# Giving out the half differences of a max search one row half at a time, in an attention mix on one core

## The chip, the core and the metric

The kernel runs on one core of one Trainium2 chip. The metric is the device time of one execution, in microseconds (us). The profile is of one execution, recorded instruction by instruction. Engines are named as the profile names them: PE is TensorE's matmuls and PEld its weight loads, ACT is ScalarE, DVE is VectorE, POOL is GpSimd, SP is SyncE.

## The reference: what is computed

Two attention branches share one input x of 2048 positions by 512 features and are mixed by a sigmoid gate. Branch A is a sliding, dilated attention: 32 heads of 16 features, each query against 8 keys, two positions apart. Branch B is a full attention with 32 query heads and one shared key head and value head. The output is the gated sum.

```python
scores = jnp.einsum("bhqd,bkd->bhqk", q, k) * (Dh ** -0.5)
p = _softmax(scores, axis=-1)
o = jnp.einsum("bhqk,bkd->bhqd", p, v)
...
return g * a + (1 - g) * b
```

The softmax of branch B needs, for every query and head, the maximum of its scores over 2048 keys (or a number near it), and finding these maxima is the work that the change is about.

## The kernel before, in words

**The work of branch B.** It is cut into 32 units (NU), each of 512 queries and four heads. The weighted part runs in 512 steps, 16 a unit: a step takes 128 keys, forms the scores of the unit by two pairs of matmuls (`exp_pair`, L487; the four heads lie in pairs of 64-row halves of the array, even in rows 0 to 63, odd in rows 64 to 127), exponentiates them with two ACT instructions (L489), and multiplies the result of the step before with the values (`weighted`, L497, eight matmul instructions a step).

**The maxima.** Before a unit's step 0 the maxima of its rows have to be known, since they are fed into the score matmul as an additional row of the queries. They are found by "fills": a score matmul of 128 queries by 512 keys, for an even or an odd head, into a bank of PSUM, and a DVE maximum over it. One row half by 512 keys is a half fill; there are 2048 of them (NF). Three forms exist:

- `fill_pair`: both halves, matmuls into the two banks of m2 (tile pm), one DVE reduce of 1024 (L357).
- `fill_one`: one half into m1 (tile ps) or po, one DVE reduce of 512 (L368).
- The difference form, which covers four half fills (two blocks of 512 keys, both heads). It uses max(a, b) = (a + b)/2 + |a - b|/2. `half_keys` and `half_parts` prepare the half sums and half differences of pairs of key blocks (kcd) once. `fill_diff` issues two half matmuls of differences (L422) into the two banks of m2, and two ACT absolute values (L432) from there into the halves of a tile dd. Two half sums follow (`fill_sum`): a half matmul (L422) into m1 for even and po for odd, and one DVE instruction (L442) that adds the absolute values to it, writes the sum back over them in dd, and keeps the maximum.

`half_sel` makes one dd tile for the projection stage; an output stage takes two tiles of the exponentials' pool (pexp) instead, and `dd.append(dd.pop(0))` turns to the other one for each difference.

**The stages.** First the keys, queries and branch A's projections are formed. From some 26 us on, the rest of the queries (14 lumps) and branch A's projections (64 lumps, L1098, each of 12 rounds; a round is one matmul in each row half) run as a stream; ACT copies each finished lump out of PSUM (L251, L252), POOL adds the halves, and a DMA on SP's queue stores every second one to ad. The difference form is used from 100 us on, when kcd is formed. From 266 us on the 512 steps run, with plain fills between the matmuls. Two output stages interrupt the steps, for eight and for four rows of the output: streams of projection matmuls (L783) in which fills run in the difference form again. The last four rows are spread over the last steps. POOL computes branch A beside all this. At most eight units' queries fit in SBUF, so fills reach only units 0 to 7 before the steps begin.

**What sets the order.** The kernel is scheduled by hand: the Python planner keeps a clock for PE, ACT and DVE (`clk`) and the time at which each bank comes free (`free`), adds its constants (T_R 0.23 for a round, 0.18 where it is a branch A round, T_LAT 0.20, T_TTR 0.66 and so on), and writes instructions in the order in which this clock says that they can run. The hardware runs each engine's queue in that order and waits on semaphores where the clock was wrong. `stream` is the planner's loop for the projection and output stages. In each pass it may give one row half to a single fill or a half sum (`single`), while the other half, or both, goes on with the stream. At the end of a pass it may issue a whole round besides: `fill_diff` if a pair of key blocks is at hand, no half sum is pending, m2 is free and DVE's clock is at most 1.2 us ahead. Half sums (`pend`) go out in order, when their bank is free and their absolute value will be ready within 0.4 us (`ready_d`). After an output stage, pending half sums are drained.

In the main loop the planner places `fill_pair` and `fill_one` by the banks' clocks; an output stage begins at a unit's start when its rows' attention is done and the fills are less than LEAD = 3 units ahead.

Of the kernel before, what the change touches and what calls it, by code (L numbers as in the profile page):

```python
# [8 lines left out]
AF = mybir.ActivationFunctionType  # L9
ALU = mybir.AluOpType  # L10
# [29 lines left out]
FMAX = 3.4028234e38  # L40
NH = NJ // 2
TO_END = 10
LEAD, M2S, M1S, E1S, PER_ROW = 3.0, 0.5, 0.3, 0.2, 20


T_R, T_LAT, T_EXP, T_RED2, T_RED1, T_W, T_TTR = 0.23, 0.20, 0.92, 1.14, 0.61, 1.21, 0.66
# [3 lines left out]
def gated_mix_kernel(ctx, tc, xt, wa, wk, wq, wo_a, wo_b, out):  # L50
    nc = tc.nc
# [20 lines left out]
    def home(v):  # L72

        return (v % NB, v - NB) if v < 2 * NB - 2 else ((v - NB) % (NB - 2), v - NB + 2)
# [3 lines left out]
    m2 = pp.tile([P, 2, 512], F32, name="pm")  # L78
    m1 = pp.tile([P, 512], F32, name="ps")
    po = pp.tile([P, 512], F32, name="po")  # L80
# [5 lines left out]
    clk = {"pe": 0.0, "act": 0.0, "dve": 0.0}  # L86

    def after(eng, ready, dur):
        clk[eng] = max(clk[eng], ready) + dur
        return clk[eng]  # L90
# [214 lines left out]
    slots = [(v, pr, t, kc) for kc in range(2) for v in range(2) for pr in range(2) for t in range(4)]  # L305
    slots += [(v, pr, t, kc) for v in range(2) for pr in range(2) for t in range(4) for kc in range(2, 4)]
    slots += [(v, pr, t, kc) for v in range(2, NU) for pr in range(2) for t in range(4) for kc in range(4)]
    half = []
    free = {"m2": 0.0, "m1": 0.0, "e0": 0.0, "e1": 0.0, "po": 0.0}
# [3 lines left out]
    def fillable():  # L313
        return bool(half) or bool(slots) and slots[0][0] < len(stacked) and stacked[slots[0][0]] <= clk["pe"]

    def unit_tile(v):
        for x in (v, v + 1):
            if x < NU and x not in left:
                mx[x] = wp.tile([P, 2, 2, 4, 4], F32, name="mx", bufs=3)
                if pe:  # L320
                    nc.gpsimd.memset(mx[x], -FMAX)
                    charge(250)
                else:
                    nc.scalar.activation(mx[x].rearrange("p b i t k -> p (b i t k)"), ident[:, 0:64], AF.Identity, scale=0.0, bias=mk[:, 6:7])
                left[x] = NF // NU
        return mx[v]

    def max_mm(dst, v, pr, t, kc, odd):
        b = 64 * odd
        nc.tensor.matmul(dst, qst[home(v)[0]][b:b + 62, pr, t * P:(t + 1) * P], kst[b:b + 62, kc * 512:(kc + 1) * 512], start=True, stop=True)  # L330
# [30 lines left out]
    def fill_one(dst=m1, key="m1"):  # L361
        if not half:
            v, pr, t, kc = slots.pop(0)
            half.extend([(v, pr, t, kc, 0), (v, pr, t, kc, 1)])
        v, pr, t, kc, odd = half.pop(0)
        m = unit_tile(v)
        max_mm(dst, v, pr, t, kc, odd)
        nc.vector.tensor_reduce(m[:, odd, pr, t, kc:kc + 1], dst, AX.X, ALU.max)  # L368
        free[key] = after("dve", after("pe", 0, T_R) + T_LAT, T_RED1) + 0.08
        filled(v, 1)  # L370


    sel, kcd, dd, pend, ready_d, formed, ended, wants = [], [], [], [], [0.0, 0.0], set(), set(), []
# [43 lines left out]
    def paired():  # L417
        return len(slots) > 1 and slots[0][3] % 2 == 0 and slots[0][3] // 2 in formed and slots[1] == slots[0][:3] + (slots[0][3] + 1,) and fillable()

    def half_mm(dst, v, pr, t, kc, x, odd):  # L420
        b = 64 * odd
        nc.tensor.matmul(dst, qst[home(v)[0]][b:b + 62, pr, t * P:(t + 1) * P], kcd[0][b:b + 62, kc // 2, x, :], start=True, stop=True)  # L422

    def fill_diff():
        v, pr, t, kc = slots.pop(0)
        slots.pop(0)
        for odd in range(2):
            half_mm(m2[:, odd, :], v, pr, t, kc, 1, odd)
        at = after("pe", 0, T_R) + T_LAT
        dd.append(dd.pop(0))  # L430
        for odd in range(2):
            nc.scalar.activation(dd[0][:, odd], m2[:, odd, :], AF.Abs)  # L432
            ready_d[odd] = after("act", at, 0.52) + 0.1
        free["m2"] = ready_d[1]
        pend.extend([(v, pr, t, kc, 0), (v, pr, t, kc, 1)])

    def fill_sum():
        v, pr, t, kc, odd = pend.pop(0)
        m = unit_tile(v)
        dst, key = ((m1, "m1"), (po, "po"))[odd]  # L440
        half_mm(dst, v, pr, t, kc, 0, odd)
        nc.vector.tensor_tensor_reduce(dd[0][:, odd], dst, dd[0][:, odd], 1.0, -FMAX, ALU.add, ALU.max, m[:, odd, pr, t, kc:kc + 1])  # L442
        free[key] = after("dve", max(clk["pe"] + T_R + T_LAT, ready_d[odd]), T_TTR) + 0.08
        filled(v, 2)

# [34 lines left out]
    pe, pexp, exped = [], {}, {}  # L480
# [251 lines left out]
    def stream(seq, mm, done, pooled):  # L732

        at, told = [0, 0], 0
        ended.clear()
        while min(at) < len(seq):
            single, odd = None, -1
            if wants and all(free[k] <= clk["pe"] + 0.1 for k in (("m1", "po") if wants[0] else ("m2",))):
                half_keys(wants.pop(0))
            if pend:  # L740
                if free[("m1", "po")[pend[0][4]]] <= clk["pe"] + 0.1 and ready_d[pend[0][4]] <= clk["pe"] + 0.4:
                    single, odd = fill_sum, pend[0][4]
            elif paired() and not half or 1 in wants:
                pass
            elif fillable() and free["m1"] <= clk["pe"] + 0.1:
                single, odd = lambda: fill_one(m1, "m1"), half[0][4] if half else 0
            elif pooled and fillable() and free["po"] <= clk["pe"] + 0.1:
                single, odd = lambda: fill_one(po, "po"), half[0][4] if half else 0
            dur = 0.0
            for b in (0, 1) if odd != 1 else (1, 0):  # L750
                if b == odd:
                    now = clk["pe"]
                    single()
                    clk["pe"] = now
                elif at[b] < len(seq):
                    dur = mm(b, seq[at[b]])
                    at[b] += 1
            after("pe", 0, dur or T_R)
            if ended or 0 in wants:
                pass  # L760
            elif paired():
                if not half and not pend and max(free["m2"], clk["dve"] - 1.2) <= clk["pe"] + 0.1:
                    fill_diff()
            elif slots and fillable() and free["m2"] <= clk["pe"] + 0.1:
                clk["pe"] = max(clk["pe"], free["m2"])
                fill_pair(m2, "m2")
            while told < min(at):
                told += 1
                done(seq[told - 1])

    def out_phase(js, n, whole_unit):

        m = 3 * (C + n)
        items = {}

        def mm(b, at):
            x, j, i = at
            if j not in items:
                items[j] = out_items(j, n)
                clk["pe"] = max(clk["pe"], free[f"e{x % 2}"])  # L780
            st, mv = items[j][i]
            h = slice(64 * b, 64 * b + 64)
            nc.tensor.matmul(eb[x % 2][:, b, :], st()[h], mv[h], start=(i == 0), stop=(i == m - 1))  # L783
            return T_R

        def done(at):
            x, j, i = at
            if i % 4 == 3:
                run_tasks()
                run_pool()  # L790
            if x == len(js) - 1 and i == m - 5:
                ended.add(1)
            if x == 0 and i == 1:
                turn(j, 1)
            if x == 0 and i == 6:
                later.pop(j)()
            if i == 3 * n and j != js[-1]:
                prepare(js[x + 1], n)
            if i == m - 5 and j != js[-1]:
                turn(js[x + 1], 1 - x % 2)  # L800
            if i == m - 1:
                out_store(j, x % 2)
                if j != js[-1]:
                    later.pop(js[x + 1])()

        if whole_unit:
            formed.update((0, 1))
            free["po"] = max(free["po"], clk["dve"] + 0.1)
            dd[:] = [px.tile([P, 2, 512], F32, name="pexp", bufs=6) for _ in range(2)]
        stream([(x, j, i) for x, j in enumerate(js) for i in range(m)], mm, done, False)  # L810
        while pend:
            odd = pend[0][4]
            clk["pe"] = max(clk["pe"], free[("m1", "po")[odd]], ready_d[odd] - 0.3)
            fill_sum()
            clk["pe"] += T_R
        settle("sum", 0)
        formed.clear()
# [329 lines left out]
    for s in range(NS + 1):  # L1147
# [11 lines left out]
        v = min(x[0][0] for x in (half, slots, [(NU,)]) if x)  # L1159
# [114 lines left out]
```

## Time and profile before

| | |
|---|---|
| median of 3 runs | 1475.5 us (1475.44 to 1475.64) |
| profiled execution | 1475.43 us |
| span, first to last instruction | 1473.6 us |
| granted TensorE clock | 0.999 |
| projection stage with differences | 100 to 266 us |
| steps before the first output stage | 266 to 846 us |
| output stages | 846 to 914 us and 1185 to 1222 us |
| difference absolute values (L432) | 164 in dd, 108 in pexp |

A line of the page's groups reads: line of the kernel, engine, operation, output tile <- input tiles, shape, count | busy us, mean ns of one | idle time of the engine before them, and what ended it. A line of the windows reads: stretch, its length, then per engine busy us and count of instructions, then the granted clock, the share of the DMA engines and GB/s. A line of the timeline reads: start, length, engine, line, operation, tiles, count of merged instructions, and idle time before with its releaser.

### The profile page before, as it was taken

To read this page: it belongs to the slowest core of one execution; us is meant where nothing else is said; L and a number is where in the kernel's file an instruction comes from. 1 tells how busy PE (TensorE), PEld (TensorE's weight loads), DVE (VectorE), ACT (ScalarE), POOL (GpSimd) and SP (SyncE) were. 2 spreads that over 40 slices of the span, in tenths; PEclk is the share of its full clock that TensorE was granted. 3 is DMA by queue.
4 is the path that set the end of the run, shared out by engine and by line. 5 is a ranking of instruction groups with operands and counts; after the bars stand their busy time and mean duration, and the time that the engine had idled before them with its cause. 6 is when DMAs were issued, how large, how long until landed. Compare 5 with 4: busy or idle time off the path is not lost.

```text
span 1473.6 us, 29548 instructions
## 1 busy us (share of the span) xinstructions
PE 1461.7 (99%) x10996; PEld 708.0 (48%) x10996; DVE 1193.9 (81%) x1855; ACT 1274.5 (86%) x1646; POOL 1032.6 (70%) x1828
## 2 busy tenths in 40 slices
PE   9999999999999999999999999999999999999998
PEld 5999889533333333333333376333333364333333
DVE  6976667789888888888898878899888878889712
ACT  5468988899999999999999978999999988999986
POOL 7876988887888979888889898888888330111220
PEclk9999999999999999999999999999999999999999
DMA  6754323121220211202112121120120000000110
GB/s 224 209 151 136 93 88 120 34 85 42 66 80 7 85 60 42 71 12 71 45 38 77 36 64 67 42 71 26 57 71 12 12 27 16 13 1 2 29 31 30
DMA packets 54080, 89.86 MB, mean 61 GB/s; under 512 B 18800, under 2 KB 35232, under 8 KB 49712
## 3 DMA queue, kind: packets, MB, share of 16 engines
q1 hardware_dynamic: 46928, 48.99, 11.4%
q0 software_dynamic: 6432, 37.94, 7.8%
q8 instruction: 86, 1.41, 0.4%
q10 hardware_dynamic: 576, 1.05, 0.2%
q14 instruction: 58, 0.48, 0.1%
HBM read 60.07 MB, written 27.35 MB: 59 GB/s over the span
## 4 chain that ended last, share of the span: by engine, by line
PE 91%; ACT 3%; POOL 3%; issue 1%; DVE 1%; DMA 1%; DVEq 0%; POOLq 0%; ACTq 0%
PE po L497 35%; PE pe L487 23%; PE pm L330 8%; PE ps L330 7%; PE pe L1098 7%; PE pe L783 4%; PE pm L422 2%; PE ps L422 1%; PE pm L851 1%; ACT dd L432 1%; PE po L422 1%; POOL qlo L222 1%; POOL qraw L215 1%; PE pe L185 1%; DMA xraw<-xt 1%
## 5 line engine op out<-in xcount | busy, mean ns | idle before, releaser
L489 ACT ACTIVATE pexp<-pe 128x1024 f32<-128x1024 f32 x1022 | 989.5, 1022 | 93.0 <-PE pe L487 90.8
L357 DVE TENSOR_REDUCE mx<-pm 128x2 f32<-128x1024 f32 x495 | 605.8, 1224 | 117.6 <-PE pm L330 113.8
L497 PE MATMUL po<-pexp,vst 128*32 128x512 f32 x4096 | 545.7, 605 | 0.0
L487 PE MATMUL pe<-qst,kst 64*128 64x512 f32 x1916 | 434.5, 447 | 0.4 <-ACT pexp L489 0.3
L487 PEld LDWEIGHTS pe<-qst,kst 64*128 64x128 f32 x1916 | 179.7, 183 | 473.7 <-ACT pexp L489 467.8
L368 DVE TENSOR_REDUCE mx<-ps 128x1 f32<-128x512 f32 x481 | 327.1, 680 | 3.7 <-PE ps L330 3.7
L330 PE MATMUL pm<-kst,qst 62*128 62x512 f32 x945 | 192.0, 396 | 0.3 <-DVE mx L357 0.3
L561 POOL TENSOR_TENSOR pr<-aext 128x256 f32<-128x256 f32 x256 | 182.5, 738 | 2.2 <-DMA aext<-ad 1.9
L330 PE MATMUL ps<-kst,qst 62*128 62x512 f32 x455 | 180.0, 396 | 0.2 <-DVE mx L442 0.2
L621 POOL TENSOR_TENSOR oa<-oa,av 128x256 f32<-128x256 f32 x224 | 164.1, 732 | 15.1
L497 PEld LDWEIGHTS po<-pexp,vst 128*32 128x32 f32 x4096 | 80.8, 108 | 178.2 <-issue 169.1
L618 POOL TENSOR_TENSOR av<-aext,lg 128x256 f32<-128x256 f32 x224 | 139.3, 622 | 12.7
L1098 PE MATMUL pe<-wah,xh 64*128 64x384 f32 (+1 forms) x504 | 109.8, 338 | 0.4 <-ACT gate L255 0.4
L1098 PE MATMUL pe<-wal,xh 64*128 64x384 f32 (+1 forms) x504 | 110.1, 337 | 0.0
L1098 PE MATMUL pe<-wah,xl 64*128 64x384 f32 (+1 forms) x504 | 109.9, 337 | 0.0
L432 ACT ACTIVATE dd<-pm 128x512 f32<-128x512 f32 x164 | 91.0, 608 | 17.8 <-PE pm L422 11.3
L442 DVE CUSTOM_DVE_ANT_0 dd<-ps,dd 128x512 f32<-128x512 f32 x82 | 56.7, 692 | 55.1 <-PE ps L422 28.9
L330 PEld LDWEIGHTS pm<-kst,qst 62*128 62x128 f32 x945 | 92.0, 187 | 2.8 <-DVE mx L357 1.0
L330 PEld LDWEIGHTS ps<-kst,qst 62*128 62x128 f32 x455 | 85.0, 187 | 5.5 <-DVE mx L368 1.7
L567 POOL TENSOR_TENSOR tr<-pr 128x512 f32<-128x512 f32 x64 | 81.7, 1277 | 4.1
L567 POOL TENSOR_TENSOR tr<-tr 128x256 f32<-128x256 f32 (+1 forms) x128 | 72.4, 566 | 8.3
L524 POOL TENSOR_TENSOR rl<-rl,gate_t 128x16 f32<-128x16 f32 x31 | 6.8, 220 | 100.4 <-DVE rl L518 99.9
(215 smaller groups left out, 1896.2 us busy)
## 6 DMA issues: line engine op xcount, KB each, us to landing
aext<-ad POOLq DMA_DIRECT2D x32, 1056.0 KB, 5.5
ad<-stage SPq DMA_DIRECT2D x32, 384.0 KB
qst<-qd SPq DMA_DIRECT2D x60, 128.0 KB
xraw<-xt SPq DMA_DIRECT2D x16, 256.0 KB
qd<-qhi SPq DMA_DIRECT2D x16, 256.0 KB
qd<-qlo SPq DMA_DIRECT2D x16, 256.0 KB
qst<-qd SPq DMA_DIRECT2D x60, 64.0 KB
qst<-ml SPq DMA_DIRECT2D x216, 2.0 KB
```

Of the source, the lines that this page charges most:

```text
L330: nc.tensor.matmul(dst, qst[home(v)[0]][b:b + 62, pr, t * P:(t + 1) * P], kst[b:b + 62, kc * 512:(kc + 1) * 512], start=True, stop=True)
L357: nc.vector.tensor_reduce(m[:, :, pr, t, kc], dst, AX.X, ALU.max)
L368: nc.vector.tensor_reduce(m[:, odd, pr, t, kc:kc + 1], dst, AX.X, ALU.max)
L432: nc.scalar.activation(dd[0][:, odd], m2[:, odd, :], AF.Abs)
L487: nc.tensor.matmul(bank[:, odd, :], kst[b:b + 64, kt * P:(kt + 1) * P], qst[home(u)[0]][b:b + 64, pr, :], start=True, stop=True)
L489: nc.scalar.activation(e, bank, AF.Exp, scale=SCALE)
L497: nc.tensor.matmul(po[32 * i:32 * i + 32, :], vst[:, kt, :], pexp[s, i // 2][:, i % 2, :], start=(kt == 0), stop=(kt == NJ - 1))
L561: nc.gpsimd.tensor_mul(pr[:, k], q, e[:, o:o + NH, AC:2 * AC])
L567: nc.gpsimd.tensor_add(nx, cur[:, :, 0:n], cur[:, :, n:2 * n])
L618: nc.gpsimd.tensor_mul(av, e[:, o:o + NH, 2 * AC:].rearrange("p j (h d) -> p j h d", d=DH), lg[:, w].unsqueeze(3).to_broadcast([P, NH, AG, ...
L621: nc.gpsimd.tensor_add(ao, ao, av)
L1098: nc.tensor.matmul(front[2 if x == last else x % 2][0][:, b, :n], l[h], r[h], start=(i == 0), stop=(i == 3 * C - 1))
```

## The change

`fill_diff` no longer issues both halves. It issues one: the even half opens a pair (`open_group`), the odd half completes it. The new `diff_half` says which half may go: its own bank has to be free (`half_free`, by the planner's clock, with the margin M2H = 0.0), no half sum of the same half may be pending, and DVE's clock may be at most 1.6 us ahead. A half difference takes its row half's turn in a pass of the stream, like a half sum, while the other half goes on with the stream or with a half sum; before, the pair was a round of its own. A difference may thus go out while the other half's sum is pending. Each pending half sum carries the tile of its own difference (`d`) instead of using the current `dd[0]`. The absolute value is charged 0.54 instead of 0.52. At the end of an output stage an open pair is completed first.

```diff
+M2H = 0.0
...
+    open_group, half_free = [], [0.0, 0.0]
+
+    def diff_half():
+
+        if max(half_free) != free["m2"]:
+            half_free[:] = [free["m2"]] * 2
+        odd = len(open_group) and 1
+        if any(x[4] == odd for x in pend) or half_free[odd] > clk["pe"] - M2H or clk["dve"] - 1.6 > clk["pe"]:
+            return None
+        return odd
+
     def fill_diff():
-        v, pr, t, kc = slots.pop(0)
-        slots.pop(0)
-        for odd in range(2):
-            half_mm(m2[:, odd, :], v, pr, t, kc, 1, odd)
-        at = after("pe", 0, T_R) + T_LAT
-        dd.append(dd.pop(0))
-        for odd in range(2):
-            nc.scalar.activation(dd[0][:, odd], m2[:, odd, :], AF.Abs)
-            ready_d[odd] = after("act", at, 0.52) + 0.1
-        free["m2"] = ready_d[1]
-        pend.extend([(v, pr, t, kc, 0), (v, pr, t, kc, 1)])
+        if not open_group:
+            open_group.append(slots.pop(0))
+            slots.pop(0)
+            dd.append(dd.pop(0))
+            odd = 0
+        else:
+            odd = 1
+        v, pr, t, kc = open_group[0]
+        half_mm(m2[:, odd, :], v, pr, t, kc, 1, odd)
+        nc.scalar.activation(dd[0][:, odd], m2[:, odd, :], AF.Abs)
+        half_free[odd] = ready_d[odd] = after("act", clk["pe"] + T_R + T_LAT, 0.54) + 0.1
+        free["m2"] = max(half_free)
+        pend.append((v, pr, t, kc, odd, dd[0]))
+        if odd:
+            open_group.clear()
 
     def fill_sum():
-        v, pr, t, kc, odd = pend.pop(0)
+        v, pr, t, kc, odd, d = pend.pop(0)
         m = unit_tile(v)
         dst, key = ((m1, "m1"), (po, "po"))[odd]
         half_mm(dst, v, pr, t, kc, 0, odd)
-        nc.vector.tensor_tensor_reduce(dd[0][:, odd], dst, dd[0][:, odd], 1.0, -FMAX, ALU.add, ALU.max, m[:, odd, pr, t, kc:kc + 1])
+        nc.vector.tensor_tensor_reduce(d[:, odd], dst, d[:, odd], 1.0, -FMAX, ALU.add, ALU.max, m[:, odd, pr, t, kc:kc + 1])
...
             if pend:
                 if free[("m1", "po")[pend[0][4]]] <= clk["pe"] + 0.1 and ready_d[pend[0][4]] <= clk["pe"] + 0.4:
-                    single, odd = fill_sum, pend[0][4]
-            elif paired() and not half or 1 in wants:
+                    lone[pend[0][4]] = fill_sum
+            elif open_group or paired() and not half or 1 in wants:
                 pass
...
+            if open_group or paired() and not (ended or half or 0 in wants):
+                odd = diff_half()
+                if odd is not None and odd not in lone:
+                    lone[odd] = fill_diff
             dur = 0.0
-            for b in (0, 1) if odd != 1 else (1, 0):
-                if b == odd:
+            for b in sorted((0, 1), key=lambda b: b not in lone):
+                if b in lone:
                     now = clk["pe"]
-                    single()
+                    lone[b]()
                     clk["pe"] = now
                 elif at[b] < len(seq):
                     dur = mm(b, seq[at[b]])
                     at[b] += 1
             after("pe", 0, dur or T_R)
-            if ended or 0 in wants:
-                pass
-            elif paired():
-                if not half and not pend and max(free["m2"], clk["dve"] - 1.2) <= clk["pe"] + 0.1:
-                    fill_diff()
-            elif slots and fillable() and free["m2"] <= clk["pe"] + 0.1:
+            if not (ended or 0 in wants or open_group or paired()) and slots and fillable() and free["m2"] <= clk["pe"] + 0.1:
                 clk["pe"] = max(clk["pe"], free["m2"])
                 fill_pair(m2, "m2")
...
         stream([(x, j, i) for x, j in enumerate(js) for i in range(m)], mm, done, False)
+        if open_group:
+            clk["pe"] = max(clk["pe"], half_free[1], free["m2"])
+            fill_diff()
+            clk["pe"] += T_R
```

More of the change, by code (lines that the diff above doesn't have):

```diff
@@ L736, in stream @@
         while min(at) < len(seq):
-            single, odd = None, -1
+            lone = {}
             if wants and all(free[k] <= clk["pe"] + 0.1 for k in (("m1", "po") if wants[0] else ("m2",))):
@@ L741, in stream @@
                 if free[("m1", "po")[pend[0][4]]] <= clk["pe"] + 0.1 and ready_d[pend[0][4]] <= clk["pe"] + 0.4:
-                    single, odd = fill_sum, pend[0][4]
-            elif paired() and not half or 1 in wants:
+                    lone[pend[0][4]] = fill_sum
+            elif open_group or paired() and not half or 1 in wants:
                 pass
             elif fillable() and free["m1"] <= clk["pe"] + 0.1:
-                single, odd = lambda: fill_one(m1, "m1"), half[0][4] if half else 0
+                lone[half[0][4] if half else 0] = lambda: fill_one(m1, "m1")
             elif pooled and fillable() and free["po"] <= clk["pe"] + 0.1:
-                single, odd = lambda: fill_one(po, "po"), half[0][4] if half else 0
+                lone[half[0][4] if half else 0] = lambda: fill_one(po, "po")
+            if open_group or paired() and not (ended or half or 0 in wants):
+                odd = diff_half()
+                if odd is not None and odd not in lone:
+                    lone[odd] = fill_diff
             dur = 0.0
-            for b in (0, 1) if odd != 1 else (1, 0):
-                if b == odd:
+            for b in sorted((0, 1), key=lambda b: b not in lone):
+                if b in lone:
                     now = clk["pe"]
-                    single()
+                    lone[b]()
                     clk["pe"] = now
```

## The prediction, made before the changed kernel was run

> **What bounds the kernel now.** I read the page first (busy shares, chain, groups), then the windows of each stage, then the timelines of one stretch of the projection stage and one of the main loop. The page:
>
> ```profile
> span 1473.6 us, 29548 instructions
> PE 1461.7 (99%) x10996; PEld 708.0 (48%) x10996; DVE 1193.9 (81%) x1855; ACT 1274.5 (86%) x1646; POOL 1032.6 (70%) x1828
> PE 91%; ACT 3%; POOL 3%; issue 1%; DVE 1%; DMA 1%; DVEq 0%; POOLq 0%; ACTq 0%
> L432 ACT ACTIVATE dd<-pm 128x512 f32<-128x512 f32 x164 | 91.0, 608 | 17.8 <-PE pm L422 11.3
> L442 DVE CUSTOM_DVE_ANT_0 dd<-ps,dd 128x512 f32<-128x512 f32 x82 | 56.7, 692 | 55.1 <-PE ps L422 28.9
> ```
>
> TensorE is busy nearly throughout and carries 91% of the chain, so what counts is TensorE rounds and the moments when it stands still. The 164 absolute values (L432) in tile dd are 82 differences in the projection stage, from 100 to 266 us; the other 108, in tiles pexp, are 54 differences in the two output stages. Each difference (four half matmuls, two absolute values, two reduces) replaces four plain fills.
>
> The later 24 projection lumps, 192.6 to 265.3 us, from three views of that stretch (the copy line L251, the projection matmuls L1098, the absolute values L432):
>
> ```profile
> 192.60:265.30 72.70, 11.69 (x24) 1.00 0.33 102
> 192.60:265.30 72.70, 65.74 (x576) 60.59 (x576) 1.00 0.33 102
> 192.60:265.30 72.70, 42.23 (x76) 1.00 0.33 102
> 126.10:192.60 66.50, 10.78 (x23) 1.00 0.38 118
> 126.10:192.60 66.50, 36.47 (x66) 1.00 0.38 118
> ```
>
> That is 24 lumps of 3.03 us with 38 differences, 1.58 a lump; the 23 lumps before hold 33, so 71 differences in 47 lumps, 1.51 a lump. Now the timeline of two differences:
>
> ```profile
> 167.84 0.69 DVE L442 CUSTOM_DVE_ANT_0 dd<-ps,dd 128x512 f32<-128x512 f32 x1 [0.83 <-PE ps L422]
> 168.23 0.42 PE L422 MATMUL pm<-kcd,qst 62*128 62x512 f32 x2
> 168.46 0.68 DVE L442 CUSTOM_DVE_ANT_0 dd<-po,dd 128x512 f32<-128x512 f32 x1
> 168.47 0.36 PE L1098 MATMUL pe<-wah,xl 64*128 64x384 f32 x2
> 168.65 0.35 PE L1098 MATMUL pe<-wah,xh 64*128 64x384 f32 x2
> 168.69 1.10 ACT L432 ACTIVATE dd<-pm 128x512 f32<-128x512 f32 x2 [0.45 <-PE pm L422]
> 168.99 0.39 PE L422 MATMUL ps<-kcd,qst 62*128 62x512 f32 x1
> 169.53 0.69 DVE L442 CUSTOM_DVE_ANT_0 dd<-ps,dd 128x512 f32<-128x512 f32 x1 [0.38 <-PE ps L422]
> 169.83 0.19 PEld L422 LDWEIGHTS pm<-kcd,qst 62*128 62x128 f32 x2 [0.25 <-ACT dd L432]
> 169.84 0.51 PE L422 MATMUL pm<-kcd,qst 62*128 62x512 f32 x2
> 170.18 0.34 PE L1098 MATMUL pe<-wah,xl 64*128 64x384 f32 x2
> ```
>
> Three things are to be seen. **Round prices:** a pair of projection matmuls takes 0.18 us (168.47 to 168.65), a pair of 512-column fills 0.24 (168.23 to 168.47); I use 0.176 and 0.23, since some starts lie closer. The 24 lumps then need 576/2 x 0.176 + 38 x 4/2 x 0.23 = 50.7 + 17.5 = 68.2 us; of 72.7, so 4.5 us, or **0.19 us a lump, are stalls**. **Bank wait:** the second difference's weight load at 169.83 waited 0.25 us for the absolute values, which end at 168.69 + 1.10 = 169.79; its pair then costs 0.34 instead of 0.23. **The buffer chain:** the reduce that starts at 168.46 ends at 169.14; it reads and rewrites the odd half of dd. The second absolute value of the 1.10 us pair ends at 169.79, and with one lasting 0.60 (the group's mean is 608 ns) it began near 169.19: 0.05 after that reduce ended. The projection stage has one dd tile (half_sel makes one), so absolute value, reduce and next absolute value of one half form a chain. The waits of this stretch name it:
>
> ```profile
> ACT dd L432 <- DVE mx L442: 5.9, 8, 0.9
> PEld pm L422 <- ACT dd L432: 11.3, 39, 0.7
> ```
>
> The first is small because ACT usually arrives just in time.
>
> In the main loop (one step has two exponentials) the stretch between the projection and the first output stage, by exponentials and by plain fill matmuls, then two steps without fills from the timeline, and the page's row of the exponentials:
>
> ```profile
> 266.00:846.00 580.00, 528.40 (x546) 1.00 0.17 53
> 266.00:846.00 580.00, 206.15 (x791) 99.32 (x791) 1.00 0.17 53
> 269.27 3.79 ACT L489 ACTIVATE pexp<-pe 128x1024 f32<-128x1024 f32 x4
> L489 ACT ACTIVATE pexp<-pe 128x1024 f32<-128x1024 f32 x1022 | 989.5, 1022 | 93.0 <-PE pe L487 90.8
> ```
>
> 546 exponentials are 273 steps of 2.125 us with 791/273 = 2.9 half fills each. Four exponentials without fills take 3.79 us; one lasts 1.02, so the fourth starts 2.77 us after the first, 0.92 apart, 1.85 a step. So 2.9 halves cost 0.275 us, 0.095 each: **a difference made elsewhere saves the main loop 4 x 0.095 = 0.38 us**.
>
> **The change, part by part.** No instruction is added or removed in kind; the planner, which writes the order by its own clock, hands them out differently.
>
> *More differences per lump.* Now a pair is planned when pend is empty, m2 is free and the pair's two absolute values end; by the code's constants that is 1.49 us at the earliest. With the change each half waits for its own bank: 0.23 + 0.20 + 0.54 + 0.1 = 1.07, so six rounds of 0.18, with the reduces allowing 2 x 0.66 = 1.32. ACT becomes the planner's limit: in a lump of 12 rounds at 0.18 plus 0.36 a difference, it fits 0.8 of copies and 1.08 a difference: 1.08 n + 0.8 = 2.16 + 0.36 n, n = 1.89. Working one lump through by hand gave the repeating order d0, d1, five rounds later s0, then d0 and s1 in one round, d1, s0, next lump: two differences a lump, slipping one round a lump. With uncharged work (the splits of wah, branch A's exponentials) I take 1.75; bounds 1.51 (nothing gained) and 1.89. So 82 - 71 = 11 more differences in 47 lumps (0 to 18). The first lumps with wider rows plan 1.2 of copies and gain nothing that matters. TensorE: 11 x 2 x 0.23 = **+5.1 us** (0 to +8.3). The queries of eight units, 512 halves, cap this; it is not reached.
>
> *Stalls.* In that order d of the same half comes two differences after s, with 8 rounds between: three of 0.23 and five of 0.176 on that half, 1.57 us. What really has to happen between: s to its reduce 0.54 (168.99 to 169.53), reduce 0.69, 0.05, absolute value 0.60, then load and refill 0.16 (169.79 to the pair's useful start, 0.05 + 0.11): 2.04. So TensorE, which works its queue in order with both row halves behind one waiting load, stalls 0.47, about 0.5 us. The planner knows nothing of it: it charges the bank and ACT, not dd, and its gate lets the difference go with up to 1.6 us of VectorE work ahead. The slip by a round a lump relaxes it, 0.5, 0.3, 0.1; the mean is 0.3, and I add 0.02 for exposed loads: 0.32 against 0.19, 47 x 0.13 = **+6.1 us**. Bounds: no stall left, 47 x -0.19 = -8.9; every lump at 0.5, 47 x 0.31 = +14.6. Behind a waiting load stand the projection matmuls, then the copies L251 and L252, POOL's additions and the DMAs to ad; these have slack, since branch A reads ad only after a whole group of lumps.
>
> *Half sums bound to their own tile.* It matters in the output stages, with two dd tiles from pexp: no chain between successive differences there. Their views:
>
> ```profile
> 846.00:914.00 68.00, 39.20 (x72) 1.00 0.14 47
> 1185.00:1222.00 37.00, 19.65 (x36) 1.00 0.09 29
> ACT pexp L432 <- PE pm L422: 12.2, 20, 1.2
> ```
>
> 54 differences in 12 rows, 4.5 a row, and ACT idle 12.2 us for TensorE in the first. The same planner balance gives at most 5.5 a row. I take +7 (0 to +12): 7 x 0.46 = **+3.2 us** (0 to +5.5), stalls unchanged.
>
> *Given back.* 18 differences x 0.38 = **-6.8 us** in the main loop (0 to -11.4). It comes as steps with few fills: early, since only eight units' queries are loaded until step 17 and the fills run out there, and late, where the fills end sooner. The last four rows' products stay late, since they wait for unit 29. The drain of an open pair adds under 1 us per output stage, hidden in the 7.
>
> A page gives another reading of the last term. The Trainium skill, "Perfetto Trace Analysis", Identifying the Most-Contended Engine, says that matmul busy time is a bad measure and that weight-load share shows TensorE's headroom.
>
> ```profile
> 266.00:846.00 580.00, 579.63 (x4089) 210.31 (x4087) 512.66 (x644) 533.46 (x570) 494.65 (x945) 1.00 0.17 53
> ```
>
> Weight loads here are 210.31/580 = 36%, ACT 92%: were ACT the bound, fewer fills would save nothing and -6.8 would be 0. By that rule this stretch has headroom; the trace disagrees, since steps without fills ran at 1.85 against 2.125.
>
> **The sum.** 5.1 + 6.1 + 3.2 - 6.8 = +7.6 us. The profiled execution took 1475.43 (span 1473.6 and 1.8 around it), the median 1475.5: the same within 0.1. Forecast **1483.0**.
>
> **Rivals.**
>
> 1. *The stalls go* (faster). If a half really starts when its bank is free, the 0.19 a lump falls away: 5.1 - 8.9 + 3.2 - 6.8 = -7.4, **1468.0**. For it: the 39 bank waits. Against: the reduce that ends 0.05 us before the next absolute value. It decides if the reduce of a half ends before the next half's absolute value would start anyway. 0.16.
>
> 2. *Little changes.* The planner gives out no more than now, or the stalls stay at 0.19: 0 to 5.1 + 3.2 - 6.8 = +1.5, **1475.5 to 1477.0**. For it: the gain and cost of a difference (0.38 and 0.46) nearly cancel. This is also the case that the change does nothing. 0.22.
>
> 3. *The chain binds every lump* (slower still). 0.5 of stall in all 47: 5.1 + 14.6 + 3.2 - 6.8 = +16.1, **1491.6**. For it: the repeating order. Against: its slip. With it goes ACT bounding the main loop by the row above, 7.6 + 6.8 = +14.4, 1489.9. 0.17.
>
> The forecast has 0.45, of which 0.03 lies within 0.2% (about 3 us, what a measurement of this kernel can tell from no change). So faster 0.16; same 0.22 + 0.03 = 0.25; slower 0.42 + 0.17 = 0.59. The range reaches from near rival 1 to rival 3: 1469 to 1492; beyond lie parts of both, 2 in 10 together.
>
> **What would show it.** Right: more than 164 absolute values in dd; projection stage longer by some 11 us; lumps near 3.25 us; TensorE's waits for L432 well above 11.3 us; ACT's waits for the reduce L442 well above 5.9; single matmuls into pm, apart; faster steps soon after 266 us. Wrong: about 164 absolute values (the planner's limit misjudged); lumps at 3.03 with more differences (no chain); or main-loop steps still 2.125 where fills are missing. A later output stage, if its rule on the lead of fills is missed by a unit, would move work but little time.

## The result: 10% slower, and where the time went

The changed kernel takes 1622.85 us (median of 4 runs, 1621.67 to 1625.02) against 1475.47 (1475.31 to 1475.64): a ratio of 1.1001 (95% interval 1.0988 to 1.1014). The forecast was 1483.0 in a range of 1469 to 1492: the sign held, the size did not, and the range missed by 131 us. The profiled execution took 1625.02 us.

The page of the changed kernel, with the rows that answer those of before:

```profile
span 1623.1 us, 29735 instructions
PE 1512.6 (93%) x10996; PEld 711.2 (44%) x10996; DVE 1188.0 (73%) x1858; ACT 1297.9 (80%) x1664; POOL 1031.6 (64%) x1828
PE   9987677779999999999999988899999998999998
PE 82%; ACT 9%; issue 3%; POOL 2%; DVE 2%; DMA 1%; DVEq 0%; ACTq 0%; POOLq 0%
L446 ACT ACTIVATE dd<-pm 128x512 f32<-128x512 f32 x172 | 103.6, 602 | 106.8 <-DVE mx L458 59.7
L458 DVE CUSTOM_DVE_ANT_0 dd<-ps,dd 128x512 f32<-128x512 f32 x86 | 59.3, 690 | 78.0 <-PE ps L423 60.9
```

The engines have nearly the same work as before: TensorE has the same 10996 matmuls, DVE is busy for 1188 us (1194), ACT for 1298 (1275), and an absolute value still lasts 0.60. But TensorE's share fell from 99 to 93%, and ACT has 9% of the chain instead of 3%. The tenths of TensorE show where: in slices 3 to 9 (from some 80 to 365 us) and in slices 24 to 26, the projection stage and the first output stage; slice 34, near 1360 us, has the second. The windows of the projection stage, the main loop after it, and the first output stage (columns: stretch, length, PE, PEld, DVE, ACT, POOL busy with counts, clock, DMA share, GB/s):

```profile
100.00:368.00 268.00, 195.88 (x1681) 157.15 (x1680) 119.53 (x361) 153.63 (x342) 134.14 (x214) 0.97 0.22 69
368.00:945.00 577.00, 576.77 (x4065) 208.94 (x4063) 509.47 (x641) 531.24 (x568) 494.88 (x954) 1.00 0.17 53
945.00:1050.00 105.00, 85.86 (x617) 52.57 (x615) 61.46 (x173) 64.47 (x113) 68.89 (x108) 0.97 0.13 43
```

In the first stretch every engine is idle for at least a quarter of the time: PE, DVE, ACT and POOL are busy for 196, 120, 154 and 134 of 268 us. That is the mark of a chain that runs from engine to engine, not of an engine with too much to do. The waits of that stretch (us in total, times, longest) name it:

```profile
PEld pm L423 <- ACT dd L446: 110.5, 115, 1.8
PE pm L423 <- ACT dd L446: 71.7, 110, 1.5
ACT dd L446 <- DVE mx L458: 59.7, 46, 2.5
ACT dd L446 <- PE pm L423: 41.5, 69, 2.1
```

Before, the weight loads of the differences waited 11.3 us in all for absolute values. Now it is 110.5, and the matmuls themselves show 71.7 (PE's idle time, of which part lies under the loads' waits, so the two are not added). A timeline of three successive half differences:

```profile
204.58 0.60 ACT L446 ACTIVATE dd<-pm 128x512 f32<-128x512 f32 x1 [0.93 <-DVE mx L458]
...
205.23 0.18 PEld L423 LDWEIGHTS pm<-kcd,qst 62*128 62x128 f32 x1 [1.20 <-ACT dd L446]
205.23 0.50 PE L423 MATMUL pm<-kcd,qst 62*128 62x512 f32 x1 [0.83 <-ACT dd L446]
...
205.23 0.44 PE L1117 MATMUL pe<-wah,xh 64*128 64x384 f32 x1
...
205.81 0.62 ACT L446 ACTIVATE dd<-pm 128x512 f32<-128x512 f32 x1
...
206.48 0.18 PEld L423 LDWEIGHTS pm<-kcd,qst 62*128 62x128 f32 x1 [0.35 <-ACT dd L446]
...
207.02 0.60 ACT L446 ACTIVATE dd<-pm 128x512 f32<-128x512 f32 x1 [0.59 <-PE pm L423]
```

The absolute value from 204.58 ends at 205.18, the next half difference's load starts at 205.23. Its absolute value ends at 205.81 + 0.62 = 206.43, the load after it starts at 206.48. Successive half differences alternate between the two banks of m2, so each of them **waits for the other bank**, 0.05 us after it is read. Over the whole run the matmuls of 209 of the 288 half differences that follow another start 0.05 us after the end of the absolute value before them, and none earlier. In the trace of before, the odd matmul of a pair starts 1.0 to 1.9 us ahead of the end of its even half's absolute value.

The program says the same. In its instructions the waits of the projection stage's half differences are, in words:

```
into pm bank 1 -> waits for the absolute value dd[0] <- pm bank 0
into pm bank 0 -> waits for the absolute value dd[512] <- pm bank 1
```

m2 is one tile of two banks, and a matmul into either waits for the last absolute value that read the tile. dd is one tile too, but its waits name the correct half. Before, both matmuls of a difference were written ahead of both absolute values, so that the tie cost little: the second matmul had no reader of its own pair to wait for.

One more reading places the time. The starts of the exponentials, before (L489) and after (L505), with min, median and max in ns, then the first and last start:

```profile
L489 ACT ACTIVATE pexp<-pe x1022: 1016/1023/1085, 266.5 to 1460.1; 128x1024 f32<-128x1024 f32 x171
```

```profile
L505 ACT ACTIVATE pexp<-pe x1022: 1015/1023/1085, 368.2 to 1609.6; 128x1024 f32<-128x1024 f32 x171
```

The first exponential comes 101.7 us later, the last 149.5 us, which is also what the span grew by (1623.1 - 1473.6). From the starts of all steps the table below is worked out: the pauses between steps around the two output stages, and the sum of the 509 other intervals.

| kernel | differences (projection + output) | first exponential | the two output pauses | other steps |
|---|---|---|---|---|
| before | 82 + 54 | 266.5 | 70.9 + 36.8 | 1084.9 |
| after | 86 + 59 | 368.2 | 106.1 + 54.4 | 1080.0 |
| e1, split | 86 + 59 | 279.8 | 73.0 + 38.0 | 1080.4 |
| e2, before split | 82 + 54 | 265.6 | 70.3 + 36.4 | 1085.0 |
| e3, before in series | 82 + 54 | 355.5 | 105.5 + 55.7 | 1085.5 |
| e4, planner told of the tie | 51 + 34 | 247.5 | 64.5 + 33.1 | see e4 |
| e5, split and two dd | 86 + 59 | 267.1 | 73.0 + 38.0 | 1080.2 |
| e7, before split and two dd | 82 + 54 | 263.5 | 70.3 + 36.3 | 1085.7 |
| e8, e1 told of dd | 74 + 58 | 258.5 | 70.0 + 36.2 | 1088.6 |
| e9, e5 told of the sum | 86 + 56 | 262.1 | 69.4 + 36.0 | 1082.3 |
| e10, e8's kernel again | 74 + 58 | 263.5 | 70.0 + 36.2 | 1088.6 |

So +101.7 in the projection stage, +52.8 in the output stages, -4.9 in the main loop.

### The profile page after: what moved, and what is told of

Its sections match the earlier page's. It is cut to its first block, busy times and chain, and to the rows that moved or that the text cites. A ratio compares the mean times of both kernels' runs of the same rounds, so it can differ in the third digit from the quotient of the medians.

```text
span 1623.1 us, 29735 instructions
## 1 busy us (share of the span) xinstructions
PE 1512.6 (93%) x10996; PEld 711.2 (44%) x10996; DVE 1188.0 (73%) x1858; ACT 1297.9 (80%) x1664; POOL 1031.6 (64%) x1828
## 4 chain that ended last, share of the span: by engine, by line
PE 82%; ACT 9%; issue 3%; POOL 2%; DVE 2%; DMA 1%; DVEq 0%; ACTq 0%; POOLq 0%
PE po L513 31%; PE pe L503 21%; PE pm L331 7%; PE ps L331 6%; PE pe L1117 5%; PE pm L423 5%; ACT dd L446 3%; PE pe L798 3%; ACT pexp L446 3%; ACT two L253 1%; PE pm L870 1%; DVE dd L458 1%; POOL qlo L223 1%; ACT stage L252 1%; POOL qraw L216 1%
## 5 line engine op out<-in xcount | busy, mean ns | idle before, releaser
L505 ACT ACTIVATE pexp<-pe 128x1024 f32<-128x1024 f32 x1022 | 989.7, 1022 | 87.9 <-PE pe L503 83.3
L369 DVE TENSOR_REDUCE mx<-ps 128x1 f32<-128x512 f32 x447 | 304.2, 681 | 2.9 <-PE ps L331 2.9
L446 ACT ACTIVATE dd<-pm 128x512 f32<-128x512 f32 x172 | 103.6, 602 | 106.8 <-DVE mx L458 59.7
L331 PE MATMUL ps<-kst,qst 62*128 62x512 f32 x426 | 168.2, 395 | 0.2 <-DVE mx L458 0.2
L1117 PE MATMUL pe<-wah,xh 64*128 64x384 f32 (+1 forms) x504 | 141.6, 355 | 0.4 <-ACT gate L256 0.4
L1117 PE MATMUL pe<-wah,xl 64*128 64x384 f32 (+1 forms) x504 | 140.7, 353 | 0.0
L1117 PE MATMUL pe<-wal,xh 64*128 64x384 f32 (+1 forms) x504 | 139.5, 352 | 0.0
L262 POOL TENSOR_TENSOR stage<-stage,two 128x384 f32<-128x384 f32 x64 | 64.3, 1004 | 95.4 <-ACT two L253 77.1
L423 PE MATMUL pm<-kcd,qst 62*128 62x512 f32 x140 | 65.5, 468 | 61.5 <-ACT dd L446 61.4
L446 ACT ACTIVATE pexp<-pm 128x512 f32<-128x512 f32 x118 | 70.6, 598 | 55.4 <-PE pm L423 31.8
L458 DVE CUSTOM_DVE_ANT_0 dd<-po,dd 128x512 f32<-128x512 f32 x86 | 59.3, 690 | 70.8 <-PE po L423 55.5
## 6 DMA issues: line engine op xcount, KB each, us to landing
qst<-qd SPq DMA_DIRECT2D x60, 128.0 KB
```

What stands on the lines that cost most here:

```text
L505: nc.scalar.activation(e, bank, AF.Exp, scale=SCALE)
L1117: nc.tensor.matmul(front[2 if x == last else x % 2][0][:, b, :n], l[h], r[h], start=(i == 0), stop=(i == 3 * C - 1))
```

## The experiments

**The theories.** The first (A in the expectations): the two banks of m2 are tied, and the order that the change writes turns this into the series difference, absolute value, difference, absolute value. The rival (B) is the prediction's own chain, absolute value, reduce and next absolute value through the one dd tile, far costlier than estimated.

### e1: the changed kernel with m2's banks apart

For the differences, m2 becomes two tiles of one bank; elsewhere it stays one tile of two. The order of the instructions is that of the changed kernel.

```diff
-        half_mm(m2[:, odd, :], v, pr, t, kc, 1, odd)
-        nc.scalar.activation(dd[0][:, odd], m2[:, odd, :], AF.Abs)
+        half_mm(shape_m2(True)[odd], v, pr, t, kc, 1, odd)
+        nc.scalar.activation(dd[0][:, odd], shape_m2(True)[odd], AF.Abs)
```

> The changed kernel with the same order of instructions on every engine, but for the differences m2 is given back and its two banks are taken as two tiles, so that a half difference waits for the absolute value that read its own bank, no longer for the one that read the other bank. Theory A (the program ties both banks of one tile: each half difference waits for the other half's absolute value, TensorE stands still): nearly all of the loss goes, 1470 to 1490 us, projection stage from 100 us to about 270. Theory B (the chain absolute value, reduce, absolute value in the one tile dd is what holds TensorE): little goes, above 1570 us.

Measured: 1487.48 us (1487.45 to 1487.66), a ratio of 1.0078 (1.0063 to 1.0093) to before. The tie alone is worth 1622.85 - 1487.48 = 135 us, as theory A had it; the stage ends near 280 us, some ten later than expected. The window of its projection stage, and its waits:

```profile
100.00:280.00 180.00, 178.60 (x1685) 150.57 (x1683) 119.37 (x362) 148.74 (x343) 134.22 (x215) 1.00 0.32 101
```

```profile
ACT dd L458 <- DVE mx L470: 25.4, 38, 1.1
...
PEld pm L435 <- ACT dd L458: 19.2, 55, 0.8
```

TensorE is busy for 178.6 of 180 us again and its waits for absolute values fall from 110.5 to 19.2. What is left is the chain of the prediction: ACT waits 25.4 us for the reduce, which writes dd, against 5.9 before.

The Trainium skill, "PSUM — Partial Sum Buffer", section "PSUM bank collisions raise a hardware error", asks that PSUM be guarded "by bank × quadrant" and says that two engines on different banks run clean, so that no wait is needed between a matmul into one bank and a read of another. e1 agrees: 275 of its 288 half differences that follow another load their weights before the other bank's absolute value has ended, and 135 us go.

### e2: before, with the banks apart

The same edit on the kernel before.

> The kernel before, with m2's banks as two tiles for the differences: the control for the split. Both theories: 1475 us within 3 us, since both half differences are issued ahead of both absolute values.

Measured: 1473.37 us (1472.76 to 1474.28), 0.9982 (0.9973 to 0.9992). In the old order the tie costs some 2.6 us: it only holds back the first half of the next pair until both absolute values have ended. In the trace of before no first half loads earlier, and the first half of 76 of the 136 pairs loads its weights 0.05 us after that end.

### e3: before, in series

The old kernel with one tile and the old planner; of a pair, the odd matmul is written behind the even absolute value instead of ahead of it. Nothing else moves.

```diff
-        for odd in range(2):
-            half_mm(m2[:, odd, :], v, pr, t, kc, 1, odd)
         at = after("pe", 0, T_R) + T_LAT
         dd.append(dd.pop(0))
         for odd in range(2):
+            half_mm(m2[:, odd, :], v, pr, t, kc, 1, odd)
             nc.scalar.activation(dd[0][:, odd], m2[:, odd, :], AF.Abs)
```

> The kernel before, with only the order inside a difference changed: even matmul, its absolute value, odd matmul, its absolute value, instead of both matmuls ahead of both absolute values; same planner, same number of differences. Theory A: the odd matmul now waits for the even absolute value, 0.44 to the start, 0.60 for it, 0.05 to the load and 0.1 of refill less the 0.1 of the round that it used, so about 1.1 us for each of 136 differences: 1590 to 1630 us. Theory B: dd is used as before, within 15 us of 1475.

Measured: 1617.7 us (1616.34 to 1618.46), 1.0956 (1.0938 to 1.0975). Its waits from 100 to 356 us:

```profile
PEld pm L422 <- ACT dd L431: 106.2, 82, 2.2
PE pm L422 <- ACT dd L431: 75.1, 82, 1.8
```

There are as many waits as the stage has differences. Moving one line brings nearly all of the loss into the old kernel. With e1, theory A is shown from both sides: the tie in the old order costs 2.6 us (before against e2), the change's order without the tie 12 (e1), both together 142 to 147 (e3, after).

### e4: the planner told of the tie

If the tie cannot be removed, the planner could at least know of it. One line of the changed kernel makes both banks busy until the latest absolute value ends.

```diff
-        half_free[odd] = ready_d[odd] = after("act", clk["pe"] + T_R + T_LAT, 0.54) + 0.1
+        half_free[0] = half_free[1] = ready_d[odd] = after("act", clk["pe"] + T_R + T_LAT, 0.54) + 0.1
```

> The changed kernel, one line different: after an absolute value the planner takes both banks as busy until that absolute value's end, which is what the program enforces. Theory A: TensorE's waits at the half differences fall to about the level of before and a difference takes about 2.2 us of planned time, so fewer of them: 1475 to 1500 us. Theory B: the waits stay, since dd is as before: above 1560 us.

Measured: 1582.29 us (1581.07 to 1582.89), 1.0719 (1.0703 to 1.0735). The expectation missed. TensorE's waits for absolute values from 100 to 264 us did go:

```profile
PEld pm L423 <- ACT dd L446: 3.4, 10, 0.5
```

But with half differences in series the planner finds room for 51 + 34 differences, where the kernel before has 82 + 54 and the changed kernel 86 + 59, and the main loop has to catch up. One of ten stops, each seven steps before a unit begins, where the planner lets missing fills catch up (`pause`); the window first (columns as above), then its timeline:

```profile
710.20:724.70 14.50, 7.78 (x37) 3.24 (x35) 13.11 (x12) 2.15 (x4) 6.55 (x11) 0.76 0.00 0
```

```profile
714.32 2.35 DVE L358 TENSOR_REDUCE mx<-pe 128x2 f32<-128x1024 f32 x2
...
716.58 1.22 DVE L358 TENSOR_REDUCE mx<-pm 128x2 f32<-128x1024 f32 x1
...
717.71 2.35 DVE L358 TENSOR_REDUCE mx<-pe 128x2 f32<-128x1024 f32 x2
```

DVE is busy for 13.1 of 14.5 us, one plain fill behind the other, while ACT is busy for 2.15, about two exponentials. The maxima of the next unit are due and were not found in time. From the first exponential to the last it took 1567.2 - 247.5 = 1319.7 us, against 1193.6 before; without the output pauses (97.6 against 107.7) that is +136.2 us for 51 differences less, 204 half fills: 0.67 us each, against the 0.095 that the prediction priced. The ten intervals with a stop take 122 us in all, where ten ordinary steps take 21, so they hold 101 of the 136 us. Where fills come too late, they cost DVE's time (1.22 us for a pair, 0.61 a half, by these rows) and no longer TensorE's.

### e5 and e6: two dd tiles, and the control

e1's remaining loss should be the dd chain. Two dd tiles in f32 do not fit beside the rest, so both are made in bf16 (e5); e6 has one dd tile in bf16, to tell the type from the count.

```diff
-        dd.append(pm[0].tile([P, 2, 512], F32, name="dd", bufs=1))
+        dd[:] = [pm[0].tile([P, 2, 512], mybir.dt.bfloat16, name=f"dd{k}", bufs=1) for k in range(2)]
```

> The split version of the changed kernel (two one-bank tiles, the order unchanged) with two dd tiles in the projection stage instead of one; there is room for two only as bf16, so the absolute values and sums of that stage are rounded to bf16 (the maxima become a little less exact). Theory A2 (what is left of the loss, 12 us, is the chain absolute value, reduce, absolute value in the one dd): ACT's waits for the reduce, 22.9 us in the projection stage, nearly go, and the stage gets 7 to 12 us shorter: 1475 to 1481 us. Theory C (what is left is the price of single half matmuls in TensorE's queue): 1485 to 1489 us, as with one dd.

> The control for the two dd tiles: the split version with one dd tile, as bf16. Both theories: 1487 us within 3 us, if the type by itself changes no duration.

Measured: e5 1474.89 us (1473.19 to 1476.82), 0.9994 (0.9985 to 1.0004); e6 1487.49 (1487.39 to 1487.59), 1.0078 (1.0063 to 1.0093), e1's time. So it is the second tile, not the type, that saves 12.6 us; theory A2 expected 7 to 12, theory C none. e5's waits from 100 to 264 us no longer hold ACT's wait for the reduce, and TensorE's has shrunk to

```profile
PEld pm L435 <- ACT dd L458: 1.1, 5, 0.4
```

The first exponential comes at 267.1 instead of 279.8, and nothing else in the table moves: the whole 12.7 us lies in the projection stage.

### e7: the old order with both obstacles gone

e2 with e5's two tiles.

> The kernel before with two one-bank tiles and two dd tiles in bf16. Theory A2: ACT waited only 6.0 us for the reduce here, so at most some 3 us are to be had: 1469 to 1474 us, below the 1473.4 of the split alone. Theory C: 1473.4 within 2 us.

Measured: 1471.77 us (1469.69 to 1472.16), 0.9967 (0.9954 to 0.998). The change's order (e5, 1474.89) is thus no better than the old one even where neither tie nor dd chain stands in its way: 4 + 5 more differences cost the projection stage 3.6 us and the output stages 4.4, and give back 5.5 in the main loop (the profiled executions, one of each). Neither the ranges of the two nor the intervals of their ratios overlap. Between A2 and C this run does not decide, since 1471.77 lies in both expectations; e5 against e6 did.

### e8, e9 and e10: the planner told of the chain

e8 is e1 with one dd in f32 and two additions to the planner's clock: an absolute value waits for the reduce of its half of dd, and the latency from a half sum to its reduce is 0.11 us longer, as the timelines show (0.54 from start to start against T_R + T_LAT = 0.43).

```diff
-        half_free[odd] = ready_d[odd] = after("act", clk["pe"] + T_R + T_LAT, 0.54) + 0.1
+        half_free[odd] = ready_d[odd] = after("act", max(clk["pe"] + T_R + T_LAT, dd_free[odd] if len(dd) == 1 else 0.0), 0.54) + 0.1
...
-        free[key] = after("dve", max(clk["pe"] + T_R + T_LAT, ready_d[odd]), T_TTR) + 0.08
+        free[key] = after("dve", max(clk["pe"] + T_R + T_LAT + 0.11, ready_d[odd]), T_TTR) + 0.08
+        dd_free[odd] = free[key]
```

e9 is e5 (two tiles in bf16) with the longer latency alone. e10 is e8's kernel once more.

> The split version with the planner told of the one dd: an absolute value starts no earlier than the reduce of its half of dd ends, and a sum reaches DVE 0.11 us later. It gives out 74 differences in the projection stage instead of 86, and 58 instead of 59 in the output stages. Theory A2: TensorE's waits at the half differences fall to the level of before, the projection stage ends at 262 to 268 us, and the half fills left over run in the main loop: 1474 to 1480 us. Theory C: the stage ends later than 270 us, since single half matmuls cost as much as they did, 1480 us or more.

> Two one-bank tiles, two dd tiles (bf16), and the planner told that a half sum reaches DVE 0.11 us later: 86 differences in the projection stage as in e5, 56 in the output stages instead of 59. If the waits of e5's half sums for DVE (8.1 us) are planner error, they shrink and the time is 1468 to 1473 us. If single half differences cost what the pairs do not, it stays at 1474 to 1476.

> The kernel of e8 once more beside e9, in five rounds, since its three rounds left an interval of 0.24%: 1470 to 1475 us by every theory; it tells whether it is faster than the kernel before by more than 0.2%.

Measured: e8 1472.41 us (1469.94 to 1474.71), 0.9974 (0.9962 to 0.9986); e10 1470.97 (1469.61 to 1474.65), 0.9967 (0.9955 to 0.9979); e9 1466.06 (1466.03 to 1466.19), 0.9933 (0.9921 to 0.9946), the fastest of all. Two expectations were missed on the fast side: e8 was to take 1474 to 1480 us with the projection stage ending at 262 to 268 (it ends at 258.5), e9 1468 to 1473. In f32, then, with the banks apart and the chain known to the planner, the change is 0.3% faster than before; from the old order with the banks apart (e2: 0.9982, 0.9973 to 0.9992) that can hardly be told apart, and the old order was not run with the corrected planner. e9 has the same 86 differences in the projection stage as e5 and passes through it in 5.0 us less:

```profile
L517 ACT ACTIVATE pexp<-pe x1022: 1015/1024/1081, 267.1 to 1459.2; 128x1024 f32<-128x1024 f32 x171
```

```profile
L517 ACT ACTIVATE pexp<-pe x1022: 1015/1024/1080, 262.1 to 1450.7; 128x1024 f32<-128x1024 f32 x171
```

These are e5's and e9's exponentials: the last is 8.5 us earlier, of which 5.0 were gained before the first. The instructions are the same in kind and, in that stage, in number; only a clock that is right by 0.11 us about one latency writes them in another order.

Not all of the 5.0 us need be the order's. e8 and e10 are one program, and their two profiled executions (1469.94 and 1474.65 us) differ by 5.0 us in the projection stage and by nothing after it, as the table shows. At the 1000th matmul they are level (128.0 and 127.9 us), at the 1200th e10 is 5.2 us behind (147.2 and 152.4). Between these lie two small DVE instructions that compute the gate, first in e8, then in e10:

```profile
130.01 0.17 DVE L287 TENSOR_SCALAR gate<-gate 128x16 f32<-128x16 f32 x1
135.85 0.71 DVE L289 TENSOR_SCALAR gate<-gate 128x16 f32<-128x16 f32 x1
```

```profile
129.98 3.65 DVE L287 TENSOR_SCALAR gate<-gate 128x16 f32<-128x16 f32 x1
139.59 2.88 DVE L289 TENSOR_SCALAR gate<-gate 128x16 f32<-128x16 f32 x1
```

While they last, the reduces behind them wait, and TensorE stands still at a half sum for 1.90 and 1.31 us. Why they last longer in one execution is not shown. e5's profile has one of 2.41 us, e9's none over 0.3, so a part of the 5.0 us may be of this kind. That e9 is the faster program stands without the profiles: its slowest run, 1466.19, is 7.0 us below e5's fastest, 1473.19.

## Why the prediction was wrong, point by point

- **What bounds the main loop: right; the price of a fill there: too low.** A difference saves the main loop 0.38 us by the prediction; 9 more ones (after, e1) brought 4.5 to 4.9 us, some 0.5 each, and e8, with 4 fewer than before, needed 3.7 us more, 0.9 each. Were ACT the bound there, nothing would have come back. The price of a round (0.23, so 0.46 a difference) was not measured by itself: without tie and dd chain, 9 more differences cost 8.0 us (e5 against e7), 0.9 each, stalls included.
- **"With the change each half waits for its own bank: 0.23 + 0.20 + 0.54 + 0.1 = 1.07": this step failed**, and with it the size. It took the planner's view of the banks, `half_free`, for the program's, and so the term for TensorE's stalls holds only the dd chain; the wait for the other bank stands in the sum at nothing. In the program a half difference waits for the other bank's absolute value, the latest. From one half's load to the next half's load 205.23 to 206.48 passed, 1.25 us: 0.58 to the start of the absolute value, 0.62 for it, 0.05 to the load. The planner believed that the second could follow the first at once. The projection matmul behind the load stood still as well: in the trace the first one (L1117) starts at 205.23 too. The price of the tie is 101.7 - 13.3 = 88.4 us over 86 differences in the projection stage, 1.03 each, and 52.8 - 3.3 = 49.5 us over 59 in the output stages, 0.84 each. The prediction weighed the waits of the bank only as something that could become shorter (rival 1), and none of its rivals had the tie.
- **Stalls from the dd chain, +6.1 us: right mechanism, mis-sized.** e1 shows the chain alone: 13.3 us in the projection stage, of which 4 more differences account for 1.8 at the predicted 0.46, so 11.5 from stalls, inside the bounds (to +14.6) and near rival 3. A second tile takes 12.7 away (e5).
- **Eleven more differences in the projection stage, seven in the output stages: 4 and 5.** The lump worked through by hand, two differences each, did not repeat in the planner's order, which gives 86 in a stage that held 82.
- **Output stages +3.2 us:** +3.3 in e1 (73.0 + 38.0 against 70.9 + 36.8), but with 5 more differences instead of 7, so the agreement is luck. **Given back -6.8:** -4.5 in e1, as the count is smaller.
- **The sum without the tie**, +7.6, is +12.1 in e1 (1485.6 against 1473.6 in span: +12.0). Had the program tracked the banks apart, the forecast of 1483.0 would have been 4.5 us short of 1487.5, inside its range. That is luck in part: fewer differences than forecast in the projection stage (1.8 us at the predicted price, not 5.1) offset larger stalls (11.5, not 6.1). That the changed kernel is slower was forecast, but 135 of its 147 us come from the tie, which was not.
- **"What would show it":** more than 164 absolute values (172), TensorE's waits far above 11.3 and ACT's above 5.9 all came true, and in the changed kernel all three were as much signs of a mechanism that was not foreseen. The size of the waits (110.5, where the dd chain alone gives 19.2) and whose end the next load follows tell them apart.

What remains open: why the order of the change is some 3 us behind the old one when nothing stands in its way (e5 against e7) is placed in the table but not traced to single waits, and one execution of each cannot place 3 us surely where e8 and e10 differ by 5. Whether the old order would gain as much as e9 from a planner that knows the 0.11 us was not run, so e9's gain over before cannot be put down to the change.

## What to carry to other kernels

When a plan splits the use of a buffer into parts, the program's waits have to be split with it: read what the second part's first instruction waits for, and if it is the first part's reader, make two tiles of it. Where every engine is idle for a quarter of a stage or more, look for the chain from engine to engine, and check it by the distance between one end and the next start: where it is constant (0.05 us in 209 of 288 cases here), look for the wait in the program. And a tie costs little (2.6 us here) as long as all writers are issued ahead of all readers, so an order that interleaves them (one moved line in e3) is a change of cost even if no engine does more.

## What the runs showed of the hardware that was not expected

The granted clock fell in some of the stretches where TensorE stood still, but not in step with its busy share. It was 0.999 before, and 0.76 in the stop of e4 quoted above, with TensorE busy for 7.8 of 14.5 us. Two neighbouring stretches of the changed kernel, and the projection stage of e3:

```profile
200.00:225.00 25.00, 18.29 (x150) 15.01 (x152) 11.15 (x34) 14.12 (x31) 13.54 (x26) 0.93 0.15 47
225.00:250.00 25.00, 17.90 (x163) 14.53 (x165) 11.42 (x37) 16.40 (x37) 14.37 (x30) 1.00 0.25 72
```

```profile
100.00:356.00 256.00, 180.91 (x1673) 149.82 (x1671) 118.66 (x345) 153.68 (x335) 136.99 (x225) 0.99 0.23 72
```

TensorE is busy for 18.29 us in the first and for 17.90 in the second, and only the first lost clock. The Trainium skill, "TensorE: Matmul & The Clock Gate", section "Part 1: The HAM clock gate", says that a monitor gates the clock by how busy the array was recently; the stop of e4 agrees, and the two neighbouring rows, sums over 25 us, can neither show nor refute it. The lower clock is a small part of the loss: e3 lost 89.0 us up to its first exponential (355.5 against 266.5) at a mean of 0.99, and by the 0.97 of the changed kernel's projection stage an estimate is 3% of TensorE's 196 us there, 6 us of 101.7.
